# A router search moved from ScalarE to VectorE in quarters, with wider planner allowances for the first four superblocks

## Chip, cores and metric

One Trainium2 chip, one core of it. The metric is device time in microseconds (us) of one execution, lower is better. Engines are named as in the profile: PE is TensorE's matmul, PEld its weight load, DVE is VectorE, ACT is ScalarE, POOL is GpSimd, SP issues DMAs.

## The reference, cut to what matters

```python
# x: (8, 3072, 256) float32
X = fft(fft(x, axis=1), axis=2).real            # 24576 tokens of 256 features
logits = X @ w_gate                             # 8 experts, capacity cap = 24576 // 8 = 3072 tokens each
for idx in argsort(-logits.flatten()):          # greedy: best (token, expert) pair first
    tok, e = idx // 8, idx % 8
    if assigned[tok] >= 0 or counts[e] >= cap: continue
    assigned[tok] = e; counts[e] += 1
out[mask_e] = relu(x[mask_e] @ w1[e]) @ w2[e]   # 256 -> 1024 -> 256, per expert
y = ((out @ w_a) * (out @ w_b)) @ w_out         # 256 -> 1536 -> 256, all tokens
```

The greedy assignment fills one expert after another. The kernel finds, expert by expert, which expert is full next and the exact logit at which it fills, then the list of its tokens.

## The kernel before

**Stages.** The FFT stage ends some 420 us into the span. A search for the first expert (`route(0)`, run alone) follows, and then a loop over 48 superblocks of 512 tokens, six per expert (line 1366). In superblock `sb` TensorE runs the two expert layers of `sb` (`first`, `second`, lines 1150 to 1173), then the gated second network of superblock `sb - 1` (class `Glu`, lines 1208 to 1337): per column group `q` of six, seven matrix products that ScalarE and VectorE drain out of PSUM, GpSimd multiplications and subtractions, and the output products `last`. All products are made of float16 halves.

**Side work.** Beside that main work run two lists of generators, `chains` (loading, scaling and splitting of activations) and `routes` (line 1351). `route(j)` (line 1010) does for expert `j`, in this order: `choose` in four quarters of the tokens and `keys` (VectorE); eight rounds of a 16-way search for the threshold in `phase` (lines 503 to 546); a final count, prefix sums; `compact` (line 585), twelve pairs of columns that turn the mask into a list of token numbers, at whose end `ready[j]` becomes 6; and `expert_split`, which loads and splits the expert's weights. A route starts when the route before it is done.

**One round** compares every key of a partition (192) with 15 thresholds into `cmp`, counts with 24 small matmuls into `bank` (`count`, line 436), reduces on VectorE (`rt_d`, `rt_D`), passes two more small matmuls with a VectorE step after each (`rt_fl`, `rt_ni`), and forms the next thresholds `rt_th` and `base`. For the first expert `compare` (line 418) runs on VectorE in four quarters (`alone`); for the others ScalarE writes one threshold per instruction, 15 instructions of 192 keys.

**The order of instructions** on every engine is fixed when the program is built. A planner keeps an estimated clock for PE, DVE and ACT (`Meter`, line 659). At each `tick()` between pieces of main work it emits side steps as long as `fits` (line 747) allows: a VectorE step (`"d"`) if the VectorE clock is at most `slack` = `SLACK` = 0.48 us ahead of PE's, a ScalarE step (`"s"`) with `ACTSLACK` = 0.3 us, a matmul step (`"p"`) only when PE's clock has passed its input by 0.28 us. `chains` are asked before `routes`.

**Where side work is forced.** Tokens of superblock `sb + 2` are fetched in superblock `sb` at q = 3 and 4 (line 1464). `ahead` (line 1357) runs the route to the needed point first if it isn't there: `while ready.get(j, -1) < sb % 6: side.force(routes)`. For the second expert that point lies in superblock 4, at q = 3, since tokens of superblock 6 are the first of that expert. What is forced is emitted back to back, with no main work between.

Of the kernel before, what the change touches and what calls it, by code (L numbers as in the profile page):

```python
# [40 lines left out]
NEG = -3.0e38  # L41
OB = 768
OUT = -5.0e9
SLACK = 0.48
EARLY = 0.9
ACTSLACK = 0.3
AHEAD = 3
LAG = 1
EXPM = 0x7F800000
# [253 lines left out]
class Router:  # L303
# [90 lines left out]
    def keys(s, sl, assigned=False):  # L394
# [11 lines left out]
        if assigned:  # L406
            ap = s.tmp([128, NT], name="tm")[:, :H]
            nc.vector.tensor_scalar(ap, s.asg[:, sl], 0.0, OUT, op0=OP.is_gt, op1=OP.mult)
            nc.vector.tensor_add(s.hi[:, sl], m, ap)
# [65 lines left out]
    def phase(s, number, last):  # L475
        nc = s.nc
        est = s.tmp([128, 1], name="est")
        s.est = est
        if last:
            f = s.tmp([128, E], name="f")  # L480
            nc.vector.tensor_scalar(f, s.pen, -1.0, None, op0=OP.is_gt)
            nc.vector.tensor_mul(f, f, s.rev8)
            nc.vector.tensor_reduce(est, f, AX.X, OP.max)
            yield "e"
            un = s.tmp([128, NT], name="tm")
            nc.vector.tensor_scalar(un, s.asg, 0.0, None, op0=OP.is_equal)
            nc.vector.scalar_tensor_tensor(s.asg, un, est, s.asg, op0=OP.mult, op1=OP.add)
            yield "d"
            mask, tot = s.tmp([128, NT], F16, "m0"), s.tmp([128, 2], name="tot")
            nc.vector.tensor_scalar(mask, s.asg, est, None, op0=OP.is_equal, op1=OP.add, accum_out=tot[:, 0:1])  # L490
            yield from s.prefix([mask], tot[:, 0:1])
            s.cnt = s.tmp([128, NT + 1], name="cnt")
            nc.scalar.copy(s.cnt, s.pf[:, 0])
            s.gch = None
            yield "d"
            return
        v, H = s.v, NT // 4
        if number:
            for h in range(4):
                yield from s.choose(slice(h * H, h * H + H))  # L500
            yield from s.keys(slice(0, NT), True)
        bias = s.bias[:, 0]
        for r in range(8):
            step, base, begin = 16.0 ** (7 - r), s.base[r // 4], r % 4 == 0
            if r == 4:

                nc.vector.scalar_tensor_tensor(s.hi, s.hi, s.base[0], s.v.bitcast(I32), op0=OP.subtract, op1=OP.add)
                bias = s.bias[:, 4]
                yield "s"
            if number:  # L510
                yield from s.compare(s.hi, bias, False)
            elif r > 0:
                if r in (1, 4):
                    neg = s.tmp([128, NT], name="gch")
                    nc.vector.tensor_scalar(neg, s.hi, -1.0, None, op0=OP.mult)
                yield from s.compare(neg, bias, True)
            s.counting = True
            yield "p"
            s.counting = False
            c = s.count()  # L520
            yield next(c)
            if r % 4 == 0:
                nxt = s.bias[:, r + 1]
            elif r % 4 < 3:
                nxt = s.tmp([128, 16], name="next")
                nc.vector.tensor_scalar(nxt, s.bias[:, r + 1], base, None, op0=OP.subtract)
            yield from c
            cn = s.ps([128, 8])
            nc.tensor.matmul(cn, s.signs if number else s.zeros, s.D, start=True, stop=True)
            yield "d"  # L530
            fl = s.tmp([128, E], F16, "fl")
            nc.vector.tensor_tensor(fl, cn, s.r, op=OP.is_ge)
            yield "p"
            n = s.ps([128, E])
            nc.tensor.matmul(n, s.seln, fl, start=True, stop=True)
            yield "d"
            ni = s.tmp([128, 1], name="ni")
            nc.vector.tensor_reduce(ni, n, AX.X, OP.max)
            if r % 4 < 3:
                bias = s.tmp([128, 16], name="th")  # L540
                nc.vector.scalar_tensor_tensor(bias, ni.to_broadcast([128, 16]), -step, nxt, op0=OP.mult, op1=OP.add)
            if begin:
                nc.vector.tensor_scalar(base, ni, step, -2.0 ** 31 if r == 0 else 0.0, op0=OP.mult, op1=OP.add)
            else:
                nc.vector.scalar_tensor_tensor(base, ni, step, base, op0=OP.mult, op1=OP.add)
            yield "d" if r % 4 == 3 else "s"
        v, T = s.hi, s.base[1]
        ge, gt = s.cmp[:, :, 1], s.cmp[:, :, 2]
        nc.vector.tensor_scalar(gt, s.eights(v), T, None, op0=OP.is_gt)
        nc.vector.tensor_scalar(ge, s.eights(v), T, None, op0=OP.is_ge)  # L550
        yield "p"
        yield from s.count()
        cc = s.ps([128, 16])
        nc.tensor.matmul(cc[:, 0:8], s.sel0, s.D, start=True, stop=True)
        nc.tensor.matmul(cc[:, 8:16], s.sel1, s.D, start=True, stop=True)
        yield "d"
        f, rem = s.tmp([128, E], name="f"), s.tmp([128, E], name="rem")
        need, oe = s.tmp([128, 1], name="need"), s.tmp([128, E], name="oe")
        nc.vector.tensor_tensor(f, cc[:, 0:8], s.r, op=OP.is_ge)
        nc.vector.tensor_mul(f, f, s.rev8)  # L560
        nc.vector.tensor_reduce(est, f, AX.X, OP.max)
        nc.vector.tensor_sub(rem, s.r, cc[:, 8:16])
        tm, tie, m0 = s.tmp([128, NT], name="tm"), s.tmp([128, NT], F16, "tie"), s.tmp([128, NT], F16, "m0")
        tot, gch = s.tmp([128, 2], name="tot"), s.tmp([128, NT], name="gch")
        nc.vector.tensor_mul(s.eights(gch), gt, s.eights(s.ch))
        nc.vector.tensor_scalar(tm, s.ch, est, None, op0=OP.is_equal)
        nc.vector.tensor_add(gch, gch, s.asg)
        yield "e"
        nc.vector.scalar_tensor_tensor(tie, v, T, tm, op0=OP.is_equal, op1=OP.mult, accum_out=tot[:, 1:2])
        nc.vector.tensor_scalar(m0, gch, est, None, op0=OP.is_equal, op1=OP.add, accum_out=tot[:, 0:1])  # L570
        nc.vector.tensor_scalar(oe, s.rev8, est, None, op0=OP.is_equal)
        p = s.prefix([m0, tie], tot)
        yield next(p)
        nc.vector.scalar_tensor_tensor(f, oe, 0.5, rem, op0=OP.mult, op1=OP.mult, accum_out=need)
        nc.vector.scalar_tensor_tensor(s.r, oe, 1.0e9, rem, op0=OP.mult, op1=OP.add)
        nc.vector.scalar_tensor_tensor(s.pen, oe, NEG, s.pen, op0=OP.mult, op1=OP.add)
        yield from p

        s.cnt = s.tmp([128, NT + 1], name="cnt")
        nc.scalar.copy(s.cnt, s.pf[:, 0])  # L580
        nc.vector.scalar_tensor_tensor(s.cnt, s.pf[:, 1], need, s.cnt, op0=OP.min, op1=OP.add)
        s.gch = gch
        yield "d"
# [146 lines left out]
class Side:  # L730
# [3 lines left out]
    def __init__(s, meter, slack, one=False):  # L734
        s.m, s.slack, s.one, s.lists, s.at = meter, slack, one, [], {}
        s.last = None

    def step(s, gen):
        y = next(gen, None)
        s.last = y  # L740
        if y == "w":
            s.at[id(gen)] = ("w", s.m.t["pe"] + 0.5)
        else:
            s.at[id(gen)] = (y, s.m.last)
        return y is not None

    def fits(s, gen):
        t = s.m.t
        y, at = s.at.get(id(gen), ("d", 0.0))
        if y == "p":  # L750
            return at + 0.28 <= t["pe"]
        if y == "s":
            return max(t["act"], at + 0.15) <= t["pe"] + ACTSLACK and at <= max(t["pe"], t["act"] + 0.2)
        if y == "w":
            return at <= t["pe"]
        return max(t["dve"], at + 0.15) <= t["pe"] + s.slack and at <= max(t["pe"], t["dve"] + 0.2)
# [42 lines left out]
def fft_moe_glu_kernel(ctx, tc, x, wg, w1, w2, wa, wb, wo, cd, out):  # L799
    nc = Meter(tc.nc)  # L800
# [254 lines left out]
    act = ctx.enter_context(tc.tile_pool(name="act", bufs=2))  # L1055
# [295 lines left out]
    chains, routes = [], [r0] + [route(j) for j in range(1, E)]  # L1351
    side = Side(nc, SLACK)
    side.lists = [chains, routes]
# [11 lines left out]
    G = pend = None  # L1365
    for sb in range(NSB + 1):
        now[0] = sb
        more = sb < NSB
        if more:
            while sb // 6 not in whole and sb > 0:  # L1370
# [23 lines left out]
        if more:  # L1394
# [16 lines left out]
            r = rescale(sb)  # L1411
# [109 lines left out]
```

## Time and profile before

| | us |
|---|---|
| median of 3 runs | 3822.78 (3814.68 to 3826.01) |
| profiled execution, its own time | 3824.36 |
| span of that execution in the trace | 3822.6 |
| PE busy | 3593.9 (94%) |
| DVE busy | 2576.2 (67%) |
| ACT busy | 2070.5 (54%) |
| POOL busy | 1897.2 (50%) |

Times in the trace count from the first instruction. A busy PE is not PE at its peak, since the ends of pipelined matmuls are modelled; where TensorE's clock is low the same matmul counts for longer. Side work is known by its tiles: `cmp`, `bank`, `oh` and all names that begin with `rt_`.

### The profile page before, as it was taken

Reading aid. Unit: us, or ns where it says so; the run is one execution under the profiler, and the core shown is the slowest. Engines: PE = TensorE matmul, PEld = TensorE weight load, DVE = VectorE, ACT = ScalarE, POOL = GpSimd, SP = SyncE. Lnnn points to the kernel's source line nnn. Section 1 sums busy time; section 2 is a strip of 40 time slices with the busy share of each in tenths; the row PEclk is TensorE's granted clock in tenths of the full one; section 3 lists DMA queues with packets and bytes.
Section 4 is the critical chain, followed back from the end, with each engine's and each line's share of the span. In section 5 each row is a group of like instructions: output and inputs, shape, how many; then the busy total and the mean of one; then the engine's idle time right before and its main releaser. Section 6 shows DMA issues by size and latency. Waiting matters only on the chain.

```text
span 3822.6 us, 71049 instructions
## 1 busy us (share of the span) xinstructions
PE 3593.9 (94%) x27905; PEld 2695.5 (71%) x27905; DVE 2576.2 (67%) x4963; ACT 2070.5 (54%) x4837; POOL 1897.2 (50%) x2006
## 2 busy tenths in 40 slices
PE   8998689879999999999999999999999999999998
PEld 7886357647677677776776777767767777776767
DVE  5777667567667866686677766786668666565655
ACT  2434455655655566556656556556655554444443
POOL 3332145435555555464554554555546555565645
PEclk9999799979999999999999999999999999999999
DMA  6665111010011100100010001100011010101000
GB/s 171 162 177 148 39 27 25 18 39 22 24 32 37 29 20 23 48 23 23 23 45 25 24 24 25 45 24 23 23 51 42 25 24 23 29 23 29 23 17 12
DMA packets 183888, 159.33 MB, mean 42 GB/s; under 512 B 111008, under 2 KB 160224, under 8 KB 181504
## 3 DMA queue, kind: packets, MB, share of 16 engines
q1 hardware_dynamic: 132224, 63.45, 7.0%
q0 software_dynamic: 23616, 76.57, 6.2%
q10 hardware_dynamic: 27712, 14.76, 1.8%
q8 instruction: 219, 3.59, 0.4%
q14 instruction: 117, 0.96, 0.1%
HBM read 79.24 MB, written 50.33 MB: 34 GB/s over the span
## 4 chain that ended last, share of the span: by engine, by line
PE 52%; POOL 11%; DVE 10%; issue 8%; ACT 7%; DMA 0%; POOLq 0%; ACTq 0%; DVEq 0%
PE mm L724 22%; PE acc L724 16%; PE y L724 13%; POOL gL L1286 4%; POOL u L1266 3%; ACT gH L724 3%; POOL xg L1113 2%; PE bank L724 2%; DVE v L724 2%; DVE u L724 1%; DVE x1L L724 1%; DVE c L724 1%; ACT cmp L724 1%; ACT c L724 1%; DVE w L724 1%
## 5 line engine op out<-in xcount | busy, mean ns | idle before, releaser
L724 PE MATMUL y<-wot,gH 128*128 128x256 f16 x4608 | 795.5, 273 | 9.2 <-ACT gH L724 9.2
L724 PE MATMUL y<-wot,gL 128*128 128x256 f16 x2304 | 630.9, 274 | 36.0 <-POOL gL L1286 34.4
L1266 POOL TENSOR_TENSOR u<-u,v 128x512 f32<-128x512 f32 x288 | 373.3, 1296 | 418.4 <-DVE u L724 334.3
L724 PEld LDWEIGHTS <-wst 128*128 128x128 f16 x5184 | 504.9, 99 | 79.0 <-issue 9.5
L1286 POOL TENSOR_TENSOR gL<-c,gH 128x512 f16<-128x512 f32 x287 | 337.7, 1177 | 356.4 <-ACT gH L724 351.9
L724 PEld LDWEIGHTS <-gH 128*128 128x128 f16 x4608 | 448.9, 98 | 84.7 <-ACT gH L724 15.0
L1286 POOL TENSOR_TENSOR gL<-u,gH 128x512 f16<-128x512 f32 x287 | 378.5, 1319 | 213.1 <-ACT gH L724 213.1
L724 PE MATMUL mm<-xT,w1H 128*128 128x512 f16 x1536 | 462.0, 383 | 9.7 <-DMA xT<-xhl 9.7
L724 DVE SCALAR_TENSOR_TENSOR hL<-mm,hH 128x512 f16<-128x512 f32 x384 | 263.5, 687 | 297.1 <-ACT hH L724 296.5
L724 ACT ACTIVATE hH<-mm 128x512 f16<-128x512 f32 x384 | 228.9, 596 | 431.2 <-PE mm L724 414.0
L724 PE MATMUL mm<-x1H,wat 128*128 128x256 f16 x2304 | 410.7, 274 | 0.0
L724 PEld LDWEIGHTS <-wat 128*128 128x128 f16 x3456 | 337.7, 98 | 59.5
L724 PEld LDWEIGHTS <-wbt 128*128 128x128 f16 x3456 | 337.3, 98 | 48.5 <-issue 1.9
L724 ACT ACTIVATE u<-mm 128x512 f32<-128x512 f32 x288 | 171.7, 596 | 356.8 <-PE mm L724 318.5
L724 PE MATMUL acc<-x1H,wst 128*128 128x256 f16 x1920 | 341.4, 273 | 0.0
L1332 POOL DMA_INDIRECT out_dram<-ysb,si x192 | 193.5, 1008 | 270.1 <-ACT ysb L724 234.2
L724 ACT CAST gH<-u 128x512 f16<-128x512 f32 x288 | 178.1, 618 | 257.3 <-POOL u L1266 253.0
L724 PE MATMUL mm<-x1L,wat 128*128 128x256 f16 x1152 | 315.1, 274 | 0.0
L724 DVE TENSOR_TENSOR c<-c,w 128x512 f32<-128x512 f32 x288 | 289.0, 1003 | 11.9
L724 PE MATMUL acc<-hL,w2H 128*128 128x512 f16 x768 | 291.0, 379 | 4.4 <-DVE hL L724 4.4
L724 PE MATMUL mm<-xT,w1L 128*128 128x512 f16 x768 | 293.4, 382 | 0.0
L724 PE MATMUL acc<-hH,w2L 128*128 128x512 f16 x768 | 291.1, 379 | 0.0
(252 smaller groups left out, 8095.5 us busy)
## 6 DMA issues: line engine op xcount, KB each, us to landing
xt<-in_x_dram SPq DMA_DIRECT2D x64, 384.0 KB, 5.5
xs<-XO SPq DMA_DIRECT2D x24, 384.0 KB, 3.2
xs<-XO ACTq DMA_DIRECT2D x48, 192.0 KB, 5.1
dwin<-in_moe_w_a_dram POOLq DMA_DIRECT2D x12, 256.0 KB, 5.2
dwin<-in_moe_w_b_dram POOLq DMA_DIRECT2D x12, 256.0 KB, 3.8
dwin<-in_moe_w_out_dram POOLq DMA_DIRECT2D x12, 256.0 KB, 3.1
xg<-xs,gi POOLq DMA_INDIRECT x192, 2.8
out_dram<-ysb,si POOLq DMA_INDIRECT x192, 2.4
```

The source lines that it names most:

```text
L724: r = f(*args, **kw)
L1113: nc.gpsimd.indirect_dma_start(out=XG[sb][:, i], out_offset=None, in_=xrows, in_offset=bass.IndirectOffsetOnAxis(ap=gi[:, c:c + 1], axis=0))
L1266: nc.gpsimd.tensor_mul(t["u"], t["u"], t["v"])
L1286: (eng or nc.gpsimd).tensor_sub(t["L", h], t["cu"[h]], t["H", h])
L1332: st = nc.gpsimd.indirect_dma_start(out=out, out_offset=bass.IndirectOffsetOnAxis(ap=si[:, c:c + 1], axis=0), in_=ysb[:, i], in_offset=None)
```

## The change

`ALONE = 1`: the searches of the first and second expert (numbers 0 and 1) compare on VectorE in four quarters; only numbers above 1 use ScalarE. For number 1 the negated keys are made ahead of rounds 0 and 4, and the sum over partitions uses the matrix for 0/1 results instead of the one for signs. `FIRST = 1.0, 1.0`: while `sb < 4` the planner's two allowances are 1.0 us each. After that `SLACK` is 0.48 as before and `ACTSLACK` is 0.4 where it was 0.3.

```diff
+ALONE = 1
 SLACK = 0.48
 EARLY = 0.9
-ACTSLACK = 0.3
+ACTSLACK = 0.4
+FIRST = 1.0, 1.0
...
-            if number:
+            byact = number > ALONE
+            if byact:
                 yield from s.compare(s.hi, bias, False)
-            elif r > 0:
-                if r in (1, 4):
+            elif number or r > 0:
+                if r == (0 if number else 1) or r == 4:
                     neg = s.tmp([128, NT], name="gch")
                     nc.vector.tensor_scalar(neg, s.hi, -1.0, None, op0=OP.mult)
                 yield from s.compare(neg, bias, True)
...
-            nc.tensor.matmul(cn, s.signs if number else s.zeros, s.D, start=True, stop=True)
+            nc.tensor.matmul(cn, s.signs if byact else s.zeros, s.D, start=True, stop=True)
...
+        s.actslack = ACTSLACK
...
-            return max(t["act"], at + 0.15) <= t["pe"] + ACTSLACK and at <= max(t["pe"], t["act"] + 0.2)
+            return max(t["act"], at + 0.15) <= t["pe"] + s.actslack and at <= max(t["pe"], t["act"] + 0.2)
...
     for sb in range(NSB + 1):
         now[0] = sb
+        side.slack, side.actslack = FIRST if sb < 4 else (SLACK, ACTSLACK)
```

## Rows read from the trace of the kernel before

**Rows 1.** The page: span, and PE's busy tenths in 40 slices
```profile
span 3822.6 us, 71049 instructions
...
PE   8998689879999999999999999999999999999998
```

**Rows 2.** Windows of superblocks 1 to 5, and 41: length, busy per engine, PEclk, DMA
```profile
482.40:555.90 73.50, 66.61 (x465) 47.12 (x466) 44.24 (x89) 43.10 (x100) 29.92 (x31) 0.92 0.08 18
555.90:624.50 68.60, 65.78 (x520) 48.45 (x517) 61.55 (x112) 37.84 (x84) 37.45 (x38) 1.00 0.09 24
624.50:691.70 67.20, 66.50 (x552) 50.09 (x550) 43.27 (x87) 41.80 (x96) 36.32 (x38) 1.00 0.10 25
691.70:822.30 130.60, 86.44 (x695) 63.19 (x694) 56.51 (x147) 70.82 (x190) 37.50 (x40) 0.76 0.09 29
822.30:891.20 68.90, 65.26 (x498) 47.80 (x497) 63.27 (x106) 38.64 (x75) 39.78 (x39) 1.00 0.09 24
3303.70:3369.30 65.60, 64.56 (x496) 47.96 (x495) 38.78 (x67) 31.38 (x65) 37.05 (x38) 1.00 0.10 25
```

**Rows 3.** PE's timeline: last main matmul ahead of the gap, first behind it
```profile
741.90 0.27 PE L724 MATMUL acc<-x1H,wst 128*128 128x256 f16 x1
...
802.68 0.63 PE L724 MATMUL y<-wot,gH 128*128 128x256 f16 x2
```

**Rows 4.** Windows, 10 us within that gap
```profile
750.00:760.00 10.00, 2.84 (x39) 2.29 (x36) 1.65 (x9) 5.29 (x15) 0.00 (x0) 0.50 0.00 0
```

**Rows 5.** Waits, 720 to 830 us: who waited for whom, total, times, longest
```profile
PE bank L724 <- ACT cmp L724: 18.5, 4, 5.9
```

**Rows 6.** Timeline of DVE and ACT: the second expert's route, milestones in order
```profile
566.42 0.55 DVE L724 TENSOR_TENSOR rt_M<-L,pen 128x384 f32<-128x384 f32 x1
...
601.48 0.80 ACT L724 ACTIVATE cmp<-hi,c_bias 128x192 f16<-128x192 f32 x2 [2.18 <-DVE hi L724]
...
722.83 0.16 DVE L724 TENSOR_REDUCE rt_ni<-bank 128x1 f32<-128x8 f32 x1
...
770.30 0.17 DVE L724 TENSOR_REDUCE rt_ni<-bank 128x1 f32<-128x8 f32 x1 [0.26 <-PE bank L724]
...
781.86 0.42 ACT L724 ACTIVATE rt_scr<-bank,c_slot 128x192 f16<-128x192 f32 x1 [0.57 <-PE bank L724]
...
806.16 0.18 DVE L724 SCALAR_TENSOR_TENSOR si<-rt_w 128x24 int32<-128x24 f32 x1
```

**Rows 7.** Compares over the whole span, by tile `cmp`: ns minimum/median/maximum
```profile
L724 ACT ACTIVATE cmp<-hi,rt_th x540: 437/442/468, 630.4 to 2794.1; 128x192 f16<-128x192 f32 x180
...
L724 DVE TENSOR_TENSOR cmp<-rt_gch,rt_th x24: 901/902/909, 378.5 to 416.0; 128x720 f16<-128x720 f32 x24
```

**Rows 8.** DVE's timeline: first and last of seven small steps in one round
```profile
741.67 0.22 DVE L724 TENSOR_TENSOR rt_d<-bank,c_diag 128x64 f32<-128x64 f32 x1 [1.55 <-PE bank L724]
...
743.82 0.23 DVE L724 TENSOR_SCALAR rt_next<-c_bias,base 128x16 f32<-128x16 f32 x1
```

**Rows 9.** Windows: the second expert's choice and keys
```profile
566.40:601.40 35.00, 33.24 (x237) 22.82 (x236) 33.26 (x59) 16.03 (x34) 17.44 (x21) 1.00 0.13 31
```

**Rows 10.** Timeline of DVE and ACT: the third expert's route, milestones in order
```profile
1128.32 0.16 DVE L724 TENSOR_REDUCE rt_ni<-bank 128x1 f32<-128x8 f32 x1
...
1156.21 0.41 ACT L724 ACTIVATE rt_scr<-bank,c_slot 128x192 f16<-128x192 f32 x1
...
1219.71 0.18 DVE L724 SCALAR_TENSOR_TENSOR si<-rt_w 128x24 int32<-128x24 f32 x1
```

**Rows 11.** Groups by form, DVE, 857 to 907 us: busy us, mean ns, idle
```profile
L724 DVE TENSOR_TENSOR oh<-ch,c_small 128x384 f16<-128x384 f32 x4 | 4.7, 1178 | 0.1
...
L724 DVE TENSOR_REDUCE ch<-rt_M 128x48 f32<-128x384 f32 x4 | 2.2, 542 | 0.0
```

**Rows 12.** The page, costliest groups: busy us, mean ns, idle before, by releaser
```profile
L724 PE MATMUL y<-wot,gH 128*128 128x256 f16 x4608 | 795.5, 273 | 9.2 <-ACT gH L724 9.2
L724 PE MATMUL y<-wot,gL 128*128 128x256 f16 x2304 | 630.9, 274 | 36.0 <-POOL gL L1286 34.4
```

## The prediction

> **What bounds the kernel now.** I read the page first: the span, and PE's busy tenths by slice [rows 1]. PE is at nine tenths nearly everywhere behind the FFT stage, so this is a TensorE kernel and side work costs only where it makes PE wait. The dip to read lies in the superblock loop, the eighth and ninth slice, 669 to 860 us. The windows by superblock [rows 2] place it: superblocks 2, 3 and 5 take 68.6, 67.2 and 68.9 us, superblock 4 takes 130.6. Against the mean of 3 and 5, 68.05 us, it loses 62.5 us. PE's timeline shows what happens there [rows 3]: no main matmul between 741.9 and 802.7 us, 60.8 us. Within the gap ScalarE works half the time and PE little, at the lower of its two clocks, 1.2 GHz [rows 4]; the longest wait of the stretch that ends in PE is for ScalarE's compares [rows 5]. That is the forced route of the second expert. Its milestones [rows 6] are: choice from 566.4, rounds from 601.5, the fourth round's end at 722.8, the eighth's at 770.3, column pairs from 781.9, list complete at 806.2. So a round beside main work took (722.8 - 601.5) / 4 = 30.3 us, and four rounds and everything behind them were left for the point in superblock 4 where the list must be complete.
>
> **What the change removes.** 120 ScalarE compares of 0.442 us (8 rounds of 15) [rows 7], by themselves off the path; what they gate is the pace of the rounds. If the route is done before PE reaches 741.9, the whole 62.5 us goes, and the clock's recovery with it, which is inside that figure. So the term to size is how much of the route is still left at that point.
>
> **The pace of a round afterwards.** A round needs four VectorE compares of 0.902 us, 3.6 us [rows 7], and seven small steps, 1.4 us together [rows 8], so 5.0 us of VectorE. An undisturbed superblock keeps VectorE busy 38.78 of 65.60 us [rows 2], which leaves 41% for side work. The choice and keys, which are VectorE work alone, did fill it even under the old allowance: 33.26 of 35.00 us busy [rows 9]. At 41% a round takes 5.0 / 0.41 = 12.2 us. Three handovers to PE's queue can't overlap with compares; with some 60 ticks in a superblock of 65.6 us each waits up to 1.1 us. I take 14 us; the bounds are 12.2 and the old 30.3. Eight rounds: 112 us instead of 242. The two negations are under 1 us in all, and the other counting matrix has the same shape: both nothing.
>
> **The rest of the route.** Choice and keys stay at 35 us; VectorE was 95% busy there, so a wider allowance has little to give. From the eighth round's end to the first column pair the forced route took 11.6 us [rows 6], the third expert's, beside main work, 27.9 [rows 10]; with the allowance of 1.0 us I take 16, nearer the forced end because most of its steps are short and wait for the planner. From there to the complete list: 24.3 us forced [rows 6], 63.5 beside main work [rows 10]; I take 50, nearer the second, since superblock 4, where most of it falls, has the old allowance for VectorE and 0.4 instead of 0.3 us for ScalarE. Sum from the start of the choice: 35 + 112 + 16 + 50 = 213 us. From 566.4 to 741.9 there are 175.5 us. The choice may start earlier: the first expert's column pairs stand before it in superblocks 0 and 1, where ScalarE is busy 43.10 of 73.50 us [rows 2], so the wider allowance has room. Bounds are 0 and 35 us (it can't start much before superblock 1 is half done); I take 18, the middle. Left over: 213 - 175.5 - 18, about 20 us at the pace beside main work, 0.4 of the column pairs, which forced cost 0.4 x 24.3, about 10 us. **So 10 of the 62.5 us stay**, bounds 0 and 30 (the column pairs and half of the steps before them).
>
> **What it adds on the path.** First, PE's own side matmuls now stand between main matmuls instead of in the gap: four counts of 24 and their two small products each, twelve column pairs. In the gap PE was busy about 2.84 us in 10 at half clock [rows 4], so 60.8 x 0.284 = 17 us there, 8 at full clock. Second, VectorE is full in superblocks 2 to 4 instead of 2 and 5 alone, and its queue is in order: behind a compare stand the drains of PSUM (`hL`, `u`, `v`, `w`), for which PE waits, and with 1.0 us of allowance a compare may be emitted that much further ahead. Superblock 2, with VectorE busy 61.55 us, took 1.4 us more than superblock 3 with 43.27 [rows 2]; twice that, and as much again for the allowance, gives 4 us (bounds -5, since the wider allowance may also fill superblock 1, which lies 7.9 us over superblock 41, and +15). ScalarE, freed of 120 compares, releases no late main step that the rows show, so I book nothing for it. Third, `ACTSLACK` 0.4 from superblock 4 on: ScalarE side steps in the searches of experts 3 to 7 come up to 0.1 us further ahead of PE. PE's idle time put down to ScalarE is small, 9.2 us in the whole span in front of the output products and 34.4 behind GpSimd [rows 12]; I book 0, bounds -6 and +6. The later routes don't inherit a new stall: they begin where this one ends, and it ends no later in superblocks than now.
>
> Sum: 62.5 - 10 - 8 - 4 = 40.5 us gained, 3824.4 - 40.5 = 3783.9 for the profiled execution. The median of the runs lies 1.6 us below that execution: 3782.3, rounded 3782.
>
> **A rule weighed against it.** Row first: an operation of VectorE with two inputs in SBUF and 384 columns took 1.178 us on average in the third expert's choice, a reduction of the same 384 columns in the same stretch 0.542 [rows 11]; GpSimd works in both. The compares have two inputs in SBUF, and the 0.902 us was measured in the first expert's search, before the loop. The Trainium skill (SBUF — State Buffer, section Who interferes with whom) says that such an instruction contends with a GpSimd instruction that reads SBUF, and that the second to issue blocks fully until the first is done; by that rule compares would be slower in the loop than alone, and the rows agree in size. What that does to the time is the second rival.
>
> **Rivals.**
> *The stall goes altogether.* If rounds run at the floor of 12.2 us, the choice starts 35 us earlier and the column pairs take 40, the route needs 35 + 98 + 16 + 40 = 189 us of 210: done with room. Then 62.5 - 8 gives 54, and superblock 1 may return up to 5: 3764 to 3770, and I take 3767. For it: ScalarE's room in superblocks 0 and 1. Against it: superblock 4 has the old VectorE allowance.
> *Compares collide with GpSimd.* At the extra 0.64 us of [rows 11] each of 32 compares costs 20 us more VectorE, 50 us at the share of 41%. The shortfall becomes 70 us instead of 20: the column pairs and all the steps before them are forced, 24.3 + 11.6 = 36 us stay instead of 10, and 4 more are lost where GpSimd's product is held up: 3812; with half of the collisions 3797. Against it: some of those long operations stand in the busiest stretch of a superblock, while a third of each superblock has little GpSimd arithmetic.
> *Slower.* The one mechanism is the raised `ACTSLACK` in the some 31 superblocks from 5 to 35 that carry side work: if a ScalarE step ahead of a PSUM drain costs PE 1.8 us per superblock, that is 56 us, 16 more than the gain, 3838. It decides from 40.5 / 31 = 1.3 us per superblock. Against it: those superblocks lie only 1.6 to 3.3 us over the undisturbed 65.6 [rows 2], mostly with their own counting, and 0.1 us is under a quarter of one compare.
> *No effect.* The planner could reach the same point with the same four rounds left, if handovers and not compares set the 30.3 us. Then it is 3815 to 3830. Against it: 15 compares take 15 emission slots, four take four.
>
> **How the numbers follow.** A measurement of this kernel can tell about 0.3%, 11.5 us, from no change: faster means under 3811.3. Forecast 0.58 (3773 to 3793), stall gone 0.17, collisions 0.16 (3793 to 3813, a fifth of it within 0.3%), no effect 0.05, slower 0.04. Faster: 0.58 + 0.17 + 0.13 = 0.88; same 0.08; slower 0.04. The range leaves out the slower and no-effect cases, the upper part of the collisions and the lowest corner: 3761 to 3804.
>
> **What would show it.** The gap of [rows 3] shrinks to under 15 us and holds column pairs only; superblock 4 takes 75 to 85 us. In the second expert's search there are no ScalarE compares, 32 VectorE compares, rounds of 12 to 16 us, the choice starting 10 to 30 us earlier. VectorE is over 55 us busy in superblocks 2 and 3. It is wrong if the rounds stay over 20 us, if compares take over 1.3 us on average, or if superblocks 2 and 3 grow by more than 5 us each.

## The result and the profile after

The changed kernel takes 3771.81 us (median of 4 runs, 3769.76 to 3774.47), the kernel before 3823.69 us beside it. The ratio is 0.9869, 95% interval 0.9852 to 0.9886: 52 us, 1.3%, faster. The profiled execution took 3769.76 us, with a span of 3767.7, which is 54.9 us less than [rows 1].

First the page of the changed kernel, span and PE's busy tenths in 40 slices:

```profile
span 3767.7 us, 70959 instructions
...
PE   7998589999999999999999999999999999999998
```

The dip of the eighth and ninth slice [rows 1] is gone. Then the windows of superblocks 1 to 5, one row each: from and to, length, busy us of PE, PEld, DVE, ACT and POOL with instruction counts, granted clock, DMA share, GB/s. They answer to [rows 2].

```profile
485.50:553.20 67.70, 63.68 (x460) 45.11 (x461) 51.06 (x101) 42.96 (x96) 29.89 (x31) 0.97 0.08 19
553.20:629.20 76.00, 68.81 (x577) 50.37 (x576) 70.83 (x129) 31.07 (x65) 41.38 (x39) 1.00 0.10 22
629.20:706.40 77.20, 72.47 (x674) 54.52 (x672) 69.98 (x144) 33.36 (x71) 41.02 (x40) 1.00 0.16 49
706.40:773.80 67.40, 66.42 (x519) 49.88 (x517) 43.85 (x88) 40.31 (x108) 35.58 (x39) 1.00 0.12 25
773.80:840.80 67.00, 65.06 (x497) 47.67 (x495) 61.23 (x106) 39.45 (x77) 40.52 (x38) 1.00 0.11 25
```

Superblock 4 went from 130.6 to 67.4 us (-63.2), and its granted clock from 0.76 to 1.00. Superblocks 2 and 3 pay: 68.6 to 76.0 and 67.2 to 77.2 (+17.4). Superblock 1 gained 5.8 and superblock 5 1.9 us; superblock 0 took 3.7 us more and the stretch behind superblock 5 4.5 us less. With 0.6 ahead of the loop that is -63.2 + 17.4 - 5.8 - 1.9 + 3.7 - 4.5 - 0.6 = -54.9 us. The last three terms are not shown to come from the change: one execution differs from another by as much, as the section on the ScalarE allowance shows.

The second expert's route in the timeline of DVE and ACT, at the milestones of [rows 6]: choice, first compare, end of the eighth round, first column pair, complete list.

```profile
537.36 0.55 DVE L727 TENSOR_TENSOR rt_M<-L,pen 128x384 f32<-128x384 f32 x1
...
575.58 0.91 DVE L727 TENSOR_TENSOR cmp<-rt_gch,c_bias 128x720 f16<-128x720 f32 x1
...
681.06 0.16 DVE L727 TENSOR_REDUCE rt_ni<-bank 128x1 f32<-128x8 f32 x1
...
705.92 0.42 ACT L727 ACTIVATE rt_scr<-bank,c_slot 128x192 f16<-128x192 f32 x1 [0.42 <-PE bank L727]
...
760.45 0.18 DVE L727 SCALAR_TENSOR_TENSOR si<-rt_w 128x24 int32<-128x24 f32 x1
```

The route starts 29 us earlier, its rounds take (681.06 - 575.58) / 8 = 13.2 us each instead of 30.3 beside main work, and the list is complete 46 us earlier than in [rows 6]. PE's longest wait within superblock 4 (engine, what waited for what, total us, times, longest), and where it stands in PE's timeline:

```profile
PE bank L727 <- ACT rt_scr L727: 0.7, 1, 0.7
```
```profile
746.86 0.33 PE L727 MATMUL bank<-rt_dif,ob 128*128 128x196 f16 x2 [0.74 <-ACT rt_scr L727]
```

That is the ninth column pair, beside main work and 10 us ahead of the point where the list is needed. Of the gap itself nothing is left.

### The profile page after: what moved, and what is told of

Same layout as the page of the kernel before. It is cut to its first block, busy times and chain, and to the rows that moved or that the text cites. A ratio compares the mean times of both kernels' runs of the same rounds, so it can differ in the third digit from the quotient of the medians.

```text
span 3767.7 us, 70959 instructions
## 1 busy us (share of the span) xinstructions
PE 3575.4 (95%) x27905; PEld 2683.1 (71%) x27905; DVE 2597.4 (69%) x4997; ACT 2026.8 (54%) x4717; POOL 1902.9 (51%) x2006
## 4 chain that ended last, share of the span: by engine, by line
PE 49%; POOL 12%; DVE 9%; issue 9%; ACT 8%; DMA 0%; POOLq 0%; ACTq 0%; DVEq 0%
PE mm L727 21%; PE acc L727 15%; PE y L727 12%; POOL gL L1290 5%; POOL u L1270 4%; ACT gH L727 3%; POOL xg L1117 3%; PE bank L727 2%; DVE v L727 2%; DVE u L727 1%; DVE c L727 1%; ACT c L727 1%; DVE w L727 1%; ACT cmp L727 1%; ACT x1H L727 1%
## 5 line engine op out<-in xcount | busy, mean ns | idle before, releaser
L727 PEld LDWEIGHTS <-gL 128*128 128x128 f16 x2304 | 225.1, 98 | 99.0 <-POOL gL L1290 70.8
```

The source lines that it names most:

```text
L727: r = f(*args, **kw)
```

## The experiments

Theory A: two things set how much of the route is forced, the pace of the rounds (which engine compares) and the allowance (when the route starts and how closely its steps follow), so each edit alone leaves a part. Theory B: the allowance alone; theory C: the comparing engine alone. Further kernels look at the growth of superblocks 2 and 3: theory D puts it down to VectorE and GpSimd colliding at SBUF, theory E to PE's own counting and to side steps emitted ahead of the drains for which PE waits.

### The compares alone

```diff
-ACTSLACK = 0.4
-FIRST = 1.0, 1.0
+ACTSLACK = 0.3
+FIRST = SLACK, ACTSLACK
```

> Compares on VectorE, allowances as before (0.48 and 0.3 us throughout). Theory A (pace of the rounds and the earlier start both count, and each edit alone leaves part of the stall): the choice starts at 566 as before, rounds take 13 to 16 us, the column pairs and perhaps part of the steps before them are still forced; the gap in superblock 4 is 20 to 36 us and the time about 3797 (3790 to 3805). Theory B (the wider allowances set the pace, whichever engine compares): rounds stay over 20 us, time 3810 to 3822. Theory C (the engine of the compares is all that counts): no gap, time 3770 to 3780.

3801.11 us, ratio 0.9926 (0.9908 to 0.9944). The windows of superblocks 2, 3 and 4:

```profile
557.80:628.80 71.00, 66.35 (x523) 48.61 (x521) 66.50 (x120) 32.88 (x69) 38.86 (x38) 1.00 0.09 23
628.80:699.50 70.70, 68.41 (x603) 51.47 (x601) 58.67 (x110) 31.38 (x65) 38.98 (x38) 1.00 0.09 24
699.50:800.30 100.80, 79.35 (x641) 57.52 (x640) 65.77 (x149) 44.47 (x115) 38.70 (x40) 0.86 0.12 37
```

and PE's longest wait in superblock 4:

```profile
PE bank L727 <- ACT rt_scr L727: 15.7, 11, 1.7
```

The choice starts at 568 us as before, a round takes 17.2 us on average (over the 13 to 16 of theory A and under the 20 of theory B; with the wide VectorE allowance it takes 13, see below), and all twelve column pairs are forced: eleven waits for the `rt_scr` steps of the pairs. Superblock 4 is still 33 us longer than in the changed kernel. Over half of the gain is missing.

### The allowances alone

```diff
-ALONE = 1
-ACTSLACK = 0.4
+ALONE = 0
+ACTSLACK = 0.3
```

> Allowances of 1.0 us for the first four superblocks, the second expert's compares on ScalarE as before, later allowance 0.3. Theory A: the choice starts at about 537, rounds take 19 to 23 us, so the column pairs and the steps before them are forced; the gap in superblock 4 is 25 to 40 us and the time about 3800 (3793 to 3810). Theory B: no gap, time 3770 to 3780. Theory C: rounds of 27 us and more, the gap over 45 us, time 3810 to 3822.

3790.11 us, ratio 0.9904 (0.9888 to 0.9921). The window of superblock 4:

```profile
700.30:793.00 92.70, 74.52 (x587) 54.22 (x586) 52.76 (x121) 49.85 (x130) 37.59 (x40) 0.89 0.13 41
```

The choice starts at 538.6 us, the rounds take 19.4 us even on ScalarE, the pairs are forced, and superblock 4 is 25 us longer than in the changed kernel. The time is 3 us under the expected range, the mechanism is that of theory A. B and C both fall: against the 3826.14 us of the kernel before beside them, the allowances alone give 36 us, the compares alone 25, both together (3770.71 us, the second kernel of the next section) 55.

### The ScalarE allowance of 0.4 us, alone and left out

Alone it holds from the start, in the first four superblocks too:

```diff
-ALONE = 1
+ALONE = 0
...
-FIRST = 1.0, 1.0
+FIRST = SLACK, ACTSLACK
```

> Only the ScalarE allowance is raised, 0.3 to 0.4 us throughout. All theories: the gap in superblock 4 stays over 50 us. If the 4 to 5 us that the superblocks from 6 on gave back in the changed kernel come from this allowance: 3812 to 3820. If they come from the earlier start of the later routes: 3820 to 3826.

3822.68 us, ratio 0.9992 (0.9983 to 1.0002): no difference that can be measured. Within it the trade of the changed kernel shows in small: superblock 4 took 119.8 us instead of 130.6, and superblocks 1 to 3 took 6.7 us more together.

The counterpart is the changed kernel with 0.3 us from superblock 4 on:

```diff
-ACTSLACK = 0.4
+ACTSLACK = 0.3
```

> The changed kernel with the later ScalarE allowance back at 0.3 us. Theory A: no gap in superblock 4, 3772 to 3778; the superblocks from 6 on return to about 2805 us in all if the allowance gave the 4 to 5 us there, and stay at 2800 if it didn't.

3770.71 us, ratio 0.9857 (0.9840 to 0.9873), within the interval of the changed kernel and 1 us under the expected range. Up to superblock 5 its instructions are those of the changed kernel, in the same order on every engine. So its superblocks 2 and 3 show how far two executions of one program lie apart:

```profile
549.90:626.80 76.90, 69.07 (x577) 50.20 (x575) 71.36 (x129) 31.07 (x65) 41.42 (x39) 1.00 0.10 22
626.80:705.50 78.70, 72.78 (x674) 54.52 (x672) 69.57 (x144) 33.37 (x71) 39.60 (x40) 1.00 0.15 48
```

They take 155.6 us where the changed kernel took 153.2, and superblock 0 took 32.5 where it took 35.8 (32.1 before). Differences of 2 to 3 us between single traces tell nothing here.

That bears on the 4.5 us behind superblock 5. The windows from superblock 6 to the start of superblock 47, first before, then with 0.4 us throughout, the changed kernel, and the first kernel of the section on having the growth back:

```profile
891.20:3695.90 2804.70, 2723.15 (x21664) 2025.16 (x21662) 1916.91 (x3538) 1606.44 (x3625) 1511.68 (x1566) 1.00 0.11 29
```
```profile
887.70:3693.10 2805.40, 2723.18 (x21664) 2024.38 (x21662) 1909.19 (x3538) 1604.57 (x3625) 1505.93 (x1567) 1.00 0.11 29
```
```profile
840.80:3641.00 2800.20, 2718.95 (x21664) 2023.14 (x21662) 1908.19 (x3540) 1605.77 (x3625) 1508.36 (x1567) 1.00 0.11 29
```
```profile
845.90:3646.80 2800.90, 2720.42 (x21663) 2023.79 (x21662) 1906.87 (x3538) 1604.54 (x3625) 1505.53 (x1567) 1.00 0.11 29
```

The allowance changes the length by 0.7 us (before against the second) and 0.6 us (the counterpart takes 2800.8). The second and the fourth of these kernels have the same instructions in the same order on PE, VectorE, ScalarE and GpSimd from superblock 5 on, and lie 4.5 us apart all the same. So the 4.5 us behind superblock 5 can't be put down to any of the edits.

### Collisions at SBUF taken away

In the changed kernel the compares in the loop are slower than in [rows 7]. Groups by form, DVE, 575.5 to 681.3 us (busy us, mean ns, idle):

```profile
L727 DVE TENSOR_TENSOR cmp<-rt_gch,rt_th 128x720 f16<-128x720 f32 x24 | 26.3, 1113 | 0.0
...
L727 DVE TENSOR_TENSOR cmp<-rt_gch,c_bias 128x720 f16<-128x720 f32 x8 | 7.1, 902 | 0.1
```

and GpSimd's product `u` in superblocks 2 and 3 takes longer. The same view of POOL, before and then after:

```profile
L1266 POOL TENSOR_TENSOR u<-u,v 128x512 f32<-128x512 f32 x12 | 15.5, 1292 | 18.9 <-DVE u L724 17.8 <-DVE rt_ni L724 0.9
```
```profile
L1270 POOL TENSOR_TENSOR u<-u,v 128x512 f32<-128x512 f32 x12 | 18.9, 1577 | 33.1 <-DVE u L727 32.7 <-PE bank L727 0.3
```

The trace shows the collisions themselves. Ten of the 32 compares took 1.32 to 1.67 us, and each of the ten began while a subtraction of GpSimd was running; the first of them (POOL from 591.71 to 592.87, the compare from 591.96):

```profile
591.71 1.16 POOL L1290 TENSOR_TENSOR gL<-c,gH 128x512 f16<-128x512 f32 x1
```
```profile
591.96 1.67 DVE L727 TENSOR_TENSOR cmp<-rt_gch,rt_th 128x720 f16<-128x720 f32 x1
```

Where the compare began first it kept its 0.9 us, and the product `u` that began during it took 1.87 us (four times).

The experiment puts the thresholds into a free part of PSUM, so that a compare reads one operand from SBUF:

```diff
             elif number or r > 0:
+                if number and r % 4 == 0:
+                    th = s.psum[:, 400:416]
+                    nc.vector.tensor_copy(th, bias)
+                    bias = th
...
-                bias = s.tmp([128, 16], name="th")
+                bias = s.psum[:, 400:416] if number == ALONE else s.tmp([128, 16], name="th")
```

> The changed kernel, but the second expert's thresholds lie in PSUM, so that a compare has one input in SBUF instead of two (two small copies are added, in rounds 0 and 4). In the changed kernel 10 of its 32 compares took 1.32 to 1.67 us instead of 0.90, and GpSimd's product of superblocks 2 and 3 took 1.58 us on average instead of 1.29. Theory D (collisions at SBUF between VectorE and GpSimd cause the 17 us that superblocks 2 and 3 grew): all 32 compares at 0.90 to 1.0 us, GpSimd's product back at 1.3 us, superblocks 2 and 3 shorter by 6 us or more in all, 3760 to 3767. Theory E (the growth is PE's own side matmuls and the order of side steps ahead of drains): the compares even out, superblocks 2 and 3 change by under 3 us, 3769 to 3774.

3775.13 us, ratio 0.9876 (0.9859 to 0.9892). Compares by tile (ns minimum/median/maximum), GpSimd's product in superblocks 2 and 3, and the windows of these two:

```profile
L731 DVE TENSOR_TENSOR cmp<-rt_gch,bank x32: 892/897/905, 572.1 to 675.7; 128x720 f16<-128x720 f32 x32
```
```profile
L1274 POOL TENSOR_TENSOR u<-u,v 128x512 f32<-128x512 f32 x12 | 15.8, 1320 | 38.8 <-DVE u L731 37.6 <-PE bank L731 0.9 <-issue 0.3
```
```profile
549.80:625.40 75.60, 68.46 (x576) 50.33 (x574) 67.68 (x130) 31.36 (x65) 38.35 (x39) 1.00 0.10 22
625.40:706.40 81.00, 74.16 (x674) 54.95 (x672) 67.35 (x145) 33.47 (x71) 37.85 (x40) 0.98 0.15 47
```

The collisions are real and gone: no compare over 0.905 us, GpSimd's product back at 1.32 us. Yet superblocks 2 and 3 together are 156.6 us, not under the 153.2 and 155.6 of the two executions with collisions, and the time isn't shorter. Theory D falls. Theory E had said a change of under 3 us and 3769 to 3774 us; against the changed kernel's own trace it is 3.4, and the time lies 1 us above. Most of that is one wait of PE in superblock 3:

```profile
645.55 0.28 PE L731 MATMUL bank<-rt_D,c_sq 128*128 128x8 f32 x1 [2.45 <-DVE rt_D L731]
```

VectorE had stood idle for 3.3 us just before the steps that PE waits for, and no row says why. PE's instructions stand in the same order in both kernels, and PE is idle in superblocks 2 and 3 for 14.0 us here, 11.9 and 13.8 us there. So it isn't the longer VectorE steps that PE waits for. That the order of emission is what it waits for was argued, and this kernel alone doesn't show it.

### The allowance taken apart

Three kernels change `FIRST` alone: 0.7 for both, the wide one for VectorE steps alone, the wide one for ScalarE steps alone.

```diff
-FIRST = 1.0, 1.0
+FIRST = 0.7, 0.7
```

> The changed kernel with allowances of 0.7 us instead of 1.0 for the first four superblocks. Theory E: side steps stand less far ahead of drains, superblocks 2 and 3 together 3 to 8 us shorter; the route ends later and a few column pairs may be forced, gap 0 to 10 us; 3766 to 3780. Theory D: superblocks 2 and 3 as long as in the changed kernel, 3770 to 3782.

```diff
-FIRST = 1.0, 1.0
+FIRST = 1.0, ACTSLACK
```

> The changed kernel with the wide allowance for VectorE steps alone (1.0) and 0.4 for ScalarE steps in the first four superblocks. If the VectorE allowance sets the pace of choice and rounds: rounds under 15 us, the choice starts between 537 and 560, a gap of under 12 us, 3768 to 3785. If the ScalarE allowance does (through the first expert's column pairs): the choice starts at about 566, column pairs forced, 3790 to 3802.

```diff
-FIRST = 1.0, 1.0
+FIRST = SLACK, 1.0
```

> The changed kernel with the wide allowance for ScalarE steps alone (1.0) and 0.48 for VectorE steps. If the VectorE allowance sets the pace: as with the compares alone, 3790 to 3802. If the ScalarE allowance does: the choice starts at about 537, 3768 to 3785.

Measured: 3785.05 us (0.9894, 0.9877 to 0.9910), 3774.18 (0.9872, 0.9856 to 0.9889), 3783.76 (0.9895, 0.9879 to 0.9912). Superblock 1 took 73.9, 68.5 and 71.0 us. The windows of superblocks 2 to 4 with 0.7 for both:

```profile
557.00:630.90 73.90, 68.18 (x576) 50.15 (x574) 69.93 (x132) 32.14 (x68) 41.75 (x39) 1.00 0.11 23
630.90:705.40 74.50, 70.11 (x631) 52.30 (x630) 63.04 (x120) 31.39 (x65) 40.59 (x38) 1.00 0.09 22
705.40:782.90 77.50, 71.18 (x561) 53.19 (x559) 49.08 (x114) 43.20 (x115) 38.18 (x40) 0.96 0.16 49
```

wide for VectorE alone:

```profile
552.30:626.80 74.50, 69.19 (x577) 50.25 (x575) 71.17 (x133) 31.37 (x65) 38.92 (x38) 1.00 0.09 22
626.80:709.20 82.40, 74.64 (x673) 54.80 (x671) 70.55 (x145) 33.41 (x71) 39.74 (x41) 0.98 0.15 46
709.20:776.60 67.40, 66.45 (x519) 49.95 (x518) 43.86 (x88) 40.32 (x108) 35.55 (x39) 1.00 0.12 25
```

and wide for ScalarE alone:

```profile
555.30:624.50 69.20, 66.66 (x548) 49.55 (x547) 64.10 (x114) 32.69 (x69) 39.60 (x39) 1.00 0.09 24
624.50:695.10 70.60, 68.42 (x604) 51.58 (x603) 62.39 (x117) 31.59 (x65) 40.98 (x39) 1.00 0.09 23
695.10:782.00 86.90, 74.35 (x614) 55.34 (x613) 58.61 (x137) 44.13 (x115) 37.70 (x41) 0.92 0.14 43
```

PE's idle time in superblocks 2 and 3 is length minus busy. By VectorE's allowance, with compares on VectorE in all of them (the fourth row is the changed kernel; a round is the time from the first compare to the end of the eighth round, over 8):

| allowance VectorE, ScalarE | PE idle in 2 and 3 | length of 2 and 3 | round | superblock 4 |
|---|---|---|---|---|
| 0.48, 0.3 | 6.9 us | 141.7 us | 17.2 us | 100.8 us |
| 0.48, 1.0 | 4.7 | 139.8 | 16.2 | 86.9 |
| 0.7, 0.7 | 10.1 | 148.4 | 14.7 | 77.5 |
| 1.0, 1.0 | 11.9 | 153.2 | 13.2 | 67.4 |
| 1.0, 0.4 | 13.1 | 156.9 | 13.3 | 67.4 |

VectorE's allowance is the one that speeds the rounds, and PE's idle time in superblocks 2 and 3 grows with it: theory E. (The kernel without the later allowance, in these superblocks the program of the fourth row, has 13.8 us, so the last two rows don't differ.) Two things keep theory E from being shown in full. First, a wider VectorE allowance also brings more of the route into these two superblocks, 1126, 1152, 1207, 1251 and 1250 matmuls of PE by row, and no kernel separates how far ahead the steps stand from how many they are. Second, PE's waits in front of main matmuls, which theory E speaks of, don't follow the allowance: in these two superblocks they are 5.9, 2.9, 6.7, 7.4 and 5.1 us by row. The largest, for GpSimd's `gL`, is 4.7 us in the changed kernel, as long at the old allowance with the compares moved (first line) and shorter with the wide VectorE allowance alone (second line):

```profile
PE y L727 <- POOL gL L1290: 4.8, 6, 1.3
```
```profile
PE y L727 <- POOL gL L1290: 2.5, 4, 0.8
```

What does follow it are the waits in front of PE's own side matmuls (tile `bank`): 1.0, 1.8, 3.2, 4.1 and 7.4 us.

The wide VectorE allowance alone does nearly the whole: no gap, rounds of 13.3 us, and 0.9872 can't be told from the 0.9869 of the changed kernel. Its choice starts 15 us later than in the changed kernel (552.5 against 537.4) but takes 24.7 us instead of 38.2, so that the first compare comes only 1.6 us later (577.2 against 575.6). Here the reading holds by which VectorE's allowance sets the pace. Without it ScalarE's does count: alone it brings the choice forward to 536.7 us and the first compare from 604.1 to 584.8, and superblock 4 from 100.8 to 86.9 us. The two parts overlap. With 0.7 us both superblocks shorten by 4.8 us in all, as theory E has it, but 10 us of gap stay and superblock 1 is 6 us longer again, so the time lies 5 us over the expected range.

### Can the growth be had back?

Narrow VectorE allowance in superblocks 2 and 3 only; then, in a second kernel, the fetch that needs the list moved later; then 0.7 us with that:

```diff
-        side.slack, side.actslack = FIRST if sb < 4 else (SLACK, ACTSLACK)
+        side.slack, side.actslack = FIRST if sb < 2 else (SLACK, 1.0) if sb < 4 else (SLACK, ACTSLACK)
```

> The changed kernel with allowances of 1.0 and 1.0 us in superblocks 0 and 1, and 0.48 (VectorE) and 1.0 (ScalarE) in 2 and 3. Theory E (VectorE's allowance buys pace of the rounds with PE's idle time): superblock 1 stays at 68 us, superblocks 2 and 3 together go from 153 to 140 to 144 us, rounds take 15 to 17 us, and a gap of 10 to 20 us stays in superblock 4: 3770 to 3780, no better than the changed kernel. Rival (the growth of superblocks 2 and 3 is the counting itself): 2 and 3 stay over 150 us, 3775 to 3790.

```diff
+            if q == 5 and sb == 4:
+                for i in range(4):
+                    ahead(6, i)
-            if 3 <= q < 5 and sb < NSB - 2:
+            if 3 <= q < 5 and sb < NSB - 2 and sb != 4:
```

> As the kernel with narrow VectorE allowance in superblocks 2 and 3, and the fetch of superblock 6, which needs the complete list, is moved within superblock 4 from q = 3 and 4 to q = 5, some 14 us later. If the place of that fetch is what decides how much is forced: three column pairs fewer are forced, the gap is 6 us smaller, and the time is 5 to 8 us below the kernel without the move: 3763 to 3773. If the gap has another cause, the times are equal.

```diff
-... (SLACK, 1.0) if sb < 4 ...
+... (0.7, 1.0) if sb < 4 ...
```

> As the kernel with the later fetch, with 0.7 us for VectorE in superblocks 2 and 3 instead of 0.48. Theory E: superblocks 2 and 3 together 3 to 8 us longer, the gap under 6 us: 3763 to 3773. It beats the changed kernel if growth and gap are under 15 us together.

Measured: 3778.36 us (0.9883, 0.9867 to 0.9900), 3768.76 (0.9864, 0.9845 to 0.9883), 3774.95 (0.9875, 0.9856 to 0.9893). Superblocks 2 to 5 of the first:

```profile
556.20:626.40 70.20, 67.08 (x550) 49.49 (x548) 67.53 (x116) 31.68 (x65) 38.92 (x39) 1.00 0.10 24
626.40:698.00 71.60, 69.61 (x631) 52.44 (x629) 64.90 (x121) 31.47 (x65) 40.32 (x38) 1.00 0.09 23
698.00:777.10 79.10, 72.44 (x588) 54.19 (x586) 52.34 (x126) 43.17 (x115) 38.36 (x40) 0.96 0.17 48
777.10:845.90 68.80, 65.15 (x497) 47.68 (x495) 63.15 (x106) 38.64 (x75) 39.66 (x39) 1.00 0.09 24
```

and superblocks 4 and 5 of the second:

```profile
695.30:767.50 72.20, 69.94 (x587) 53.02 (x586) 48.82 (x117) 42.66 (x115) 34.98 (x37) 1.00 0.16 45
767.50:839.20 71.70, 65.57 (x498) 47.75 (x496) 62.92 (x111) 38.48 (x75) 41.71 (x42) 1.00 0.11 30
```

The first is as theory E expects: superblocks 2 and 3 take 141.8 us, a round 15.7, and 11 us stay in superblock 4. Moving the fetch takes 6.9 us out of superblock 4 and puts 2.9 into superblock 5, so its place does decide how much is forced. Of the 8.6 us between the two spans 3.7 lie ahead of the loop, where the programs are alike. The second kernel has the lowest median of all, 3 us under the changed kernel, but the interval of its ratio contains that of the changed kernel's almost wholly: it can't be told from it. With 0.7 us superblocks 2 and 3 take 149.3 us again and superblock 5 takes 74.2, at a granted clock of 0.95; the time lies 2 us over the expected range, and nothing is won. What the route costs moves between superblocks 2, 3, 4 and 5: together they take 287.6 us in the changed kernel, and 289.7, 285.7 and 294.2 in these three.

## Why the prediction was right, point by point

**The bound and the mechanism** were as told: the loss of superblock 4 [rows 2] was the forced route, and it left with it, clock and all (62.5 us booked, 63.2 measured). The time, 3771.8 us, lies in the range of 3761 to 3804 and on the side that was forecast, 10 us under the predicted 3782: between the likeliest case (own range from 3773) and the first rival (3767). In kind the first rival is what happened: no gap stayed, though none of its conditions was met (rounds of 12.2 us, a start 35 us earlier, pairs in 40 us; measured 13.2, 29 and 54.5).

**The pace of a round**, 14 us with a floor of 12.2, was 13.2. The argument behind it, the share of VectorE that main work leaves free, fits: with collisions a round needs 4 x 1.06 + 1.4 = 5.6 us of VectorE, 43% of 13.2 us, where 41% was the estimate. The runs show that the allowance is part of it: 17.2 us at the old one.

**The step that failed** is "so 10 of the 62.5 us stay". Its parts against the measured ones: choice and keys 35, 38.2; rounds 112, 105.5; from the last round to the first pair 16, 24.9 (nearer the end beside main work than the forced one); pairs 50, 54.5; sum 213, 223. The start came 29 us earlier and not 18. That these two misses cancel is luck. What did not cancel is that I held the point at 741.9 us. It lies at a place of the program, not of the clock: 741.9 - 691.7 = 50.2 us into superblock 4, which now starts at 706.4 us, so it came at 756.6, 14.7 us later, because superblocks 2 and 3 grew by more than superblock 1 gave back. The route had 756.6 - 537.4 = 219.2 us for its 223. Only the twelfth pair and the closing arithmetic of the list were left. In PE's timeline that pair's matmuls stand right behind the last main one ahead of the point, and main work goes on right behind them:

```profile
756.50 0.38 PE L727 MATMUL acc<-x1H,wst 128*128 128x256 f16 x2
756.72 0.33 PE L727 MATMUL bank<-rt_dif,ob 128*128 128x196 f16 x2
756.88 0.38 PE L727 MATMUL y<-wot,gH 128*128 128x256 f16 x2
```

So what was forced made PE wait for nothing: 0 of the 62.5 us stayed where 10 were booked.

**What it adds on the path** was booked at 12 us: 8 for PE's own side matmuls and 4 for VectorE's queue. PE's busy time in superblocks 2 and 3 grew from 132.3 to 141.3 us, 9.0, so the first term held. PE's idle time there grew from 3.5 to 11.9, 8.4: in these superblocks the second term was mis-sized by half. By PE's waits 5.2 us of it stand in front of main matmuls, the largest part behind the chain VectorE, GpSimd, PE (superblocks 2 and 3, before and after),

```profile
PE y L724 <- POOL gL L1286: 1.3, 3, 0.8
```
```profile
PE y L727 <- POOL gL L1290: 4.7, 6, 0.9
```

and 2.9 us in front of PE's own side matmuls, which the prediction didn't have; the second part is the one that follows the allowance (above). Its bound below nothing was used too: superblock 1 gave back 5.8 of its 7.9 us. The runs put that mainly down to VectorE's allowance at its full width: 68.5 us with it alone, 71.0 with ScalarE's alone, 73.3 with neither; at 0.7 us for both it was 73.9.

**Signs of being wrong.** One that the prediction had named came true: superblocks 2 and 3 grew by 7.4 and 10.0 us, over 5 each. Superblock 4, at 67.4 us, lies under the 75 to 85 expected. The mechanism stood all the same, but what it adds on the path was told too low and what it leaves of the gap too high.

**`ACTSLACK`** was booked at 0 and measured at 0; with it the slower rival falls, which needed 1.3 us per superblock. One argument against that rival was read too narrowly: the 1.6 to 3.3 us over the undisturbed superblock are those of superblocks 3 and 5, and superblock 15 of the kernel before takes 73.8 us, 8 over. **No effect** falls with the two kernels that make one edit each. **Collisions**: the compares with two inputs in SBUF averaged 1.06 us in the loop, (24 x 1.113 + 8 x 0.902) / 32, against 0.90 with one. That is 5 us more VectorE in all, a quarter of the 20 that the rival had from the third expert's choice [rows 11], and taking it away made nothing faster. The Trainium skill (SBUF — State Buffer, section Who interferes with whom) has the second to issue wait for the first. The trace agrees: the ten long compares, 1.32 to 1.67 us, began while GpSimd was at a subtraction, and where the compare began first the product took 1.87 us.

## What to carry to other kernels

Side work that a program emits between main work has a due point; look for the place where the program forces it, and cost an edit by how much is left there, with forced and unhurried pace from the trace. The point is a place in the program: every microsecond by which main work stretches also gives the side work time, so stretch and remaining gap must be solved together. Letting side work run further ahead is no free gain: here the change paid 17 us in two superblocks for 63 in a third, and without a forced point there would have been no 63 to win. Before a few microseconds of one trace are put down to an edit, look at how far two executions of the same instructions lie apart: 4.5 us here in 2800.

## What the hardware showed that I had not expected

Slower VectorE compares and slower GpSimd products, 18% and 22% longer on average with their collisions than without, cost this kernel no time that can be measured. A VectorE compare that reads its 15 thresholds per partition from PSUM instead of SBUF takes as long as one alone (897 against 902 ns) and no longer disturbs GpSimd (its product at 1.32 us, 1.29 before the change).
